# Routing's small operations shared out over a whole step of the groups, and the rows' last turns put earlier

## The chip, the cores and the metric

The kernel runs on one core of a Trainium2 chip. The metric is the device time of one execution in microseconds (us); three executions of the kernel before gave 1698.09, 1701.14 and 1708.59 us, median 1701.14 us. Engine names are those of the profile: PE (TensorE), DVE (VectorE), ACT (ScalarE), POOL (GpSimd) and SP (SyncE).

## The reference

Eight sequences of 5056 positions by 128 channels are convolved along the sequence with one filter `h`, by real FFTs of twice the length. The result, 40,448 tokens of 128, then goes through a mixture of experts with two-level routing:

```python
y = irfft(rfft(x, n=2*S, axis=1) * rfft(h, n=2*S, axis=0)[None], n=2*S, axis=1)[:, :S]
t = y.reshape(B*S, D)
g_logits = t @ w_group                       # 4 groups: take the largest, softmax weight g_w
e_logits = t @ w_expert[g]                   # 4 experts of that group: largest, softmax weight e_w
out[tok] = g_w * e_w * (relu(t[tok] @ w1[g, e]) @ w2[g, e])    # hidden size 1024, one expert per token
```

All inputs and results are float32.

## The kernel before

The convolution is a two-step Fourier transform (158 by 64 points) written as matmuls, in three rounds (`ROUNDS`): the filter and sequences 0 and 1, then sequences 2 to 4, then 5 to 7. A round has a first stage (`stage1`, 96 pieces: matmuls L419 and L426, copies and adds L437 to L443 into the resident tile `st`) and a stage of groups (`groups`). The groups come in pairs of frequencies, 40 pairs in 20 steps of two pairs. In a step PE transforms both pairs (`forward`, L520), DVE multiplies each by the filter's spectrum in two operations (`multiply`, L538: `y`, then `m`) and adds the two (`add`, L572; on POOL in the first round), and PE transforms back the two pairs of the step before (`inverse`, L588), which ACT copies into `zs` (L598) and SP stores to `zd`. Forward and inverse results share three double banks of PSUM (`pp`), which turn in order: an inverse whose bank held a forward result waits until DVE's `m` has read it.

Beside rounds 1 and 2 runs the last transform and the routing of the round before (`side`), and beside the expert blocks that follow the three rounds that of round 2. Its unit is a batch of 8 of the 64 positions. For each: two lumps (`lump`: matmuls L722 and L736 into the banks `py0` and `py1`, copied by ACT into `yT`, L743); the logits' matmuls (`lm`, L789, copied into `lT`, L794); their transposes (`lt`, L799, copied into `lg`, L803); three or four turns of rows (`rows`: transposes of `yT`, L779, copied by ACT into the rows `rw`, L780); and 41 steps of the routing's small operations, eight of them empty (`gate_math`, L895 to L986, nearly all on DVE, with four small matmuls L972 and L973). `lm`, `lt` and `rows` take `py0` and `py1` in turn, the same two banks as the lumps. The finished rows are sent to their expert's place in `srt` by single indirect transfers on POOL (`scatter`, L855), each after a tiny cast of its positions on DVE or ACT (L854).

The order of all instructions on each engine is written by hand. `run` makes one list, `main`, of (weight, function). In the groups a step is 11 entries with the weights `GW = [0, 0, 0, 0, 0, 0, 2.0, 0, 0, 0, 2.0]`; in the first stage each piece weighs 0.45, with entries of weight 0 between some. `weave` goes through `main` and, at entries that weigh something, puts in as much of the side's work as is due by its own times `t` (in slots; a batch in rounds 1 and 2 lasts 8 slots, so a slot is about half a step of the groups). Steps marked small are not put in at once but held in a list, `light`, and at each entry of weight 0 a part of them is issued:

```python
room[i] = room[i + 1] + 1 if main[i][0] == 0 else 0
...
    if w == 0:
        flush(-(-len(light) // room[i]))
```

So before the change `room[i]` is the number of weight-0 entries left in the present run of such entries, and the held steps are all out before the next weighted entry: what came due at the entry with index 6 goes out over the three entries 7 to 9, what came due at index 10 over the next six. The forwards and multiplies stand at indexes 1 to 5, the adds at 5, the inverses at 7 and 8, lumps and rows behind 6 and 10.

Of the kernel before, what the change touches and what calls it, by code (L numbers as in the profile page):

```python
# [45 lines left out]
GW = [0, 0, 0, 0, 0, 0, 2.0, 0, 0, 0, 2.0]  # L46
# [124 lines left out]
    }  # L171


def weave(main, sides):


    light = []

    def flush(n):
        for f in light[:n]:  # L180
            f()
        del light[:n]

    room = [0] * (len(main) + 1)
    for i in reversed(range(len(main))):
        room[i] = room[i + 1] + 1 if main[i][0] == 0 else 0
    for i, (w, f) in enumerate(main):
        f()
        if w == 0:
            flush(-(-len(light) // room[i]))  # L190
        for s in sides:
            if s["start"] <= i < s["end"]:
                if i == s["start"]:
                    s["done"] = 0
                    s["acc"] = s["sacc"] = 0.0
                    s["len"] = sum(w for w, _ in main[s["start"]:s["end"]])
                    s["total"] = sum(x[0] for x in s["steps"])
                s["acc"] += w / s["len"]
                while s["done"] < len(s["steps"]) and (s["sacc"] < s["acc"] * s["total"] - 1e-6 or i == s["end"] - 1):
                    sw, sf, small = s["steps"][s["done"]]  # L200
                    if small and room[i + 1] > 0 and i < s["end"] - 1:
                        light.append(sf)
                    else:
                        if small:
                            flush(len(light))
                        sf()
                    s["sacc"] += sw
                    s["done"] += 1
                if i == s["end"] - 1:
                    flush(len(light))  # L210
# [18 lines left out]
class Kernel:  # L229
# [455 lines left out]
    def side(self, r):  # L685
# [80 lines left out]
        def rows(i):  # L766

            if i == 0:
                od["rw"] = []
                od["o"] = od.get("o", -1) + 1  # L770
                while self.sends and self.sends[0][0] < 8 * r + od["o"] - 1:
                    self.send()
            if i % 2 == 0:
                od["rw"].append(cx.tile([128, RH, ROW], F32, name="rw", bufs=4))
            n = min(4, T - 4 * i)
            pt = bank()
            for j in range(n):
                k = (4 * i + j) * GP
                nc.tensor.transpose(out=pt[:, j * D:(j + 1) * D], in_=self.yT[:, k:k + GP], identity=self.ident)  # L779
            nc.scalar.copy(  # L780
                out=od["rw"][i // 2][:, 4 * i % RH:4 * i % RH + n, 0:D], in_=pt[:, 0:n * D].rearrange("p (j d) -> p j d", d=D)
            )
# [26 lines left out]
        def advance(g):  # L809
            return lambda: next(g, None)  # L810

        def both(*fs):
            return lambda: [f() for f in fs]
# [3 lines left out]
        for o in range(N2 // 8):  # L817
            math = {}
            ops = self.gate_math(od, math, b0 * S + o * 8, T, nu, REST if r < 2 else REST2)
            sends = [self.scatter(math, k, GP if k < T - 1 else last, r, T) for k in range(T)]  # L820
            if r < 2:
                t = 8 * o
                at.append((t, lump(2 * o), False))
                at.append((t + 3, lump(2 * o + 1), False))
                at.append((t + 4.7, both(lm, lambda: rows(0)), False))
                at.append((t + 6.4, both(lt, lambda: rows(1)), False))
                at.append((t + 9.5, both(*more), False))
                at += [(t + 6.5 + 5.6 * k / (NMATH + REST), advance(ops), True) for k in range(NMATH + REST)]
                at.append((t + 12.15, lambda o=o, s=sends: self.sends.extend((8 * r + o, f) for f in s), True))
            else:  # L830

                t = 6 * o
                at.append((t, lump(2 * o), False))
                at.append((t + 2, lump(2 * o + 1), False))
                at.append((t + 3, both(lm, lambda: rows(0)), False))
                at.append((t + 4, both(lt, lambda: rows(1)), False))
                at.append((t + 5, both(*more), False))
                at += [(t + 4.02 + 3.3 * k / (NMATH + REST2), advance(ops), True) for k in range(NMATH + REST2)]
                at.append((t + 7.4, lambda o=o, s=sends: self.sends.extend((8 * r + o, f) for f in s), True))
# [758 lines left out]
    def run(self):  # L1598
        tc = self.tc
        with ExitStack() as ctx:  # L1600
            self.pools(ctx)
            with ExitStack() as c2:
# [10 lines left out]
                def add(f, w=0.0):  # L1613
                    main.append((w, f))
# [17 lines left out]
                for r in range(3):  # L1632
                    if r == 1:
                        add(self.share)
                    pre, steps = gr[r]
                    rest = late(r - 1) if r > 0 else []
                    n = len(s1[r][1])
                    t0 = self.table_0()
                    for k, f in enumerate(s1[r][1]):
                        add(f, W_S1)  # L1640
                        if r > 0 and k % 2 == 1:
                            add(self.send)
                        if r == 0:
                            add(advance(more))
                        if r == 2 and ("end", 0) in mark:
                            add(advance(t0))
                        if k >= 1:
                            for g in rest[RP * k - RP:RP * k]:
                                add(g)
                        if k == SIDE0 and r > 0:  # L1650
                            add(side[r - 1][0])
                        if k == max(SIDE0 + SIDEG, END0 if r == 2 else 0) and r > 0:
                            mark["start", r - 1] = len(main)
                            if r == 2:
                                mark["end", 0] = len(main)
                        if k >= n - PRE and (k - n) % 5 == 0:
                            add(advance(pre))
                    if r > 0:
                        add(lambda: None, W_END)
                    for p in range(0, NQ, 2):  # L1660
                        for w, f in steps[p // 2]:
                            add(f, w)
                        if p >= NQ - LOAD1:
                            add(advance(s1[r + 1][0] if r < 2 else early))
                add(turn)
                add(lambda: self.ffn_first(0))
                rest = late(2)
# [3 lines left out]
                for k, f in enumerate(steps):  # L1671
# [35 lines left out]
                        add(lambda i=m * n // TAKE: self.take(i))  # L1707
                weave(main, [
                    dict(start=mark["start", r], end=mark["end", r], steps=side[r][1]) for r in range(3)
                ])  # L1710
                self.ffn_tail()


# [25 lines left out]
```

## Time and profile before

| | before |
|---|---|
| timed runs, median (lowest, highest) | 1701.14 us (1698.09, 1708.59) |
| profiled execution, own time / span | 1700.13 us / 1698.3 us |
| PE busy | 1630.5 us, 96% of the span |
| DVE busy | 1302.5 us, 77% |
| ACT busy | 1046.8 us, 62% |
| POOL busy | 773.3 us, 46% |
| mean granted clock of PE | 0.991 |

By the lines at work the profile falls into these stretches: the first round to about 137 us; then round 1's first stage to 200 us and its groups to 357 us; round 2's first stage to 445 us and its groups, with the turn to the experts, to 625 us; then expert blocks to the end. A wait row names engine, tile and line, what was waited for, the total in us, how many times, and the longest. A timeline row has the start in us, the duration in us, the instruction, and in brackets the idle time before it and what ended that.

### The profile page before, as it was taken

The page shows a single profiled execution, that of the slowest core. Times are in us where ns is not written, and L with a number is a line of the kernel's source. Part 1 is how long each engine was busy: PE and PEld are TensorE (multiplying, and loading weights), DVE is VectorE, ACT ScalarE, POOL GpSimd, SP SyncE. Part 2 cuts the span into 40 slices and gives each one's busy share as a digit, 9 for nine tenths or more (in the row PEclk, how much of TensorE's full clock was granted, in tenths as well). Part 3 has the DMA queues.
Part 4 walks back from the last instruction along what each step waited for, and adds up shares of the span by engine and source line. Part 5 has one row for each costly group of instructions (what it writes and reads, how often), then busy time and mean ns, then how long its engine had stood idle before and what let it go on. Part 6 is the DMA issues. An engine that isn't in the chain of part 4 may idle for free. (4 is left out here: it accounts for less than half of the span.)

```text
span 1698.3 us, 50924 instructions
## 1 busy us (share of the span) xinstructions
PE 1630.5 (96%) x18317; PEld 1275.8 (75%) x18317; DVE 1302.5 (77%) x3092; ACT 1046.8 (62%) x2461; POOL 773.3 (46%) x742
## 2 busy tenths in 40 slices
PE   8998999989899989999999999999999999999996
PEld 7676755557665557888778887888888888879986
DVE  6554698975788886777777788888887787878875
ACT  5564544544545456666666676777777776657764
POOL 1452233442555553254554454446565663334443
PEclk9999999999999999999999999999999999999998
DMA  7797678888798976566655544567555774444554
GB/s 210 224 295 223 191 243 263 274 245 217 200 289 280 287 227 172 165 177 179 177 164 173 158 139 129 153 197 219 161 161 152 213 220 139 126 132 145 164 160 139
DMA packets 278001, 330.36 MB, mean 195 GB/s; under 512 B 31863, under 2 KB 210304, under 8 KB 277720
## 3 DMA queue, kind: packets, MB, share of 16 engines
q1 hardware_dynamic: 248856, 270.93, 54.6%
q0 software_dynamic: 20608, 41.79, 7.2%
q10 hardware_dynamic: 8256, 14.10, 3.0%
q8 instruction: 152, 2.49, 0.7%
q14 instruction: 129, 1.06, 0.2%
HBM read 230.35 MB, written 96.86 MB: 193 GB/s over the span
## 5 line engine op out<-in xcount | busy, mean ns | idle before, releaser
L855 POOL DMA_INDIRECT srt<-rw,pos x320 | 345.3, 1079 | 391.4 <-DVE pos L854 116.2
L1422 POOL DMA_INDIRECT out<-orow,at x176 | 187.8, 1067 | 254.1 <-ACT at L1420 226.8
L1422 POOL DMA_INDIRECT out<-orow,sids x92 | 94.1, 1022 | 126.1 <-DVE orow L1389 89.4
L538 DVE TENSOR_TENSOR y<-pp,hg 128x768 f32<-128x768 f32 (+1 forms) x120 | 103.6, 864 | 54.3 <-ACT hg L528 32.3
L598 ACT COPY zs<-pp 128x768 f32<-128x768 f32 (+1 forms) x118 | 85.3, 723 | 81.0 <-PE pp L588 40.5
L588 PE MATMUL pp<-y,cg 64*64 64x384 f32 (+1 forms) x1472 | 116.4, 444 | 12.1 <-DVE m L538 8.0
L1357 DVE SCALAR_TENSOR_TENSOR h0l<-px,h0h 128x512 fp32r<-128x512 f32 (+1 forms) x109 | 73.7, 676 | 59.3 <-ACT h0h L1356 58.4
L520 PE MATMUL pp<-st,cg 64*64 64x192 f32 (+1 forms) x1556 | 114.4, 404 | 1.2 <-PE pp L520 0.6
L1356 ACT ACTIVATE h0h<-px 128x512 fp32r<-128x512 f32 (+1 forms) x109 | 63.9, 587 | 80.6 <-PE px L1353 72.5
L438 DVE TENSOR_TENSOR st<-pp,odd 128x320 f32<-128x320 f32 x96 | 46.9, 489 | 77.2 <-ACT odd L437 76.9
L538 DVE TENSOR_TENSOR m<-pp,hg 128x768 f32<-128x768 f32 (+1 forms) x120 | 102.9, 857 | 2.1 <-ACT hg L530 2.1
L1357 DVE SCALAR_TENSOR_TENSOR h2l<-px,h2h 128x512 fp32r<-128x512 f32 (+1 forms) x112 | 75.5, 674 | 31.0 <-ACT h2h L1356 29.9
L588 PEld LDWEIGHTS pp<-y,cg 64*64 64x64 f32 x1472 | 55.4, 133 | 52.4 <-issue 27.6
L722 PEld LDWEIGHTS py<-ig,zm 126*64 126x64 f32 x2048 | 75.0, 139 | 24.6 <-issue 8.2
L743 ACT COPY yT<-py 128x474 f32<-128x474 f32 (+1 forms) x96 | 44.3, 514 | 77.3 <-PE py L736 70.9
L1357 DVE SCALAR_TENSOR_TENSOR h3l<-px,h3h 128x512 fp32r<-128x512 f32 (+1 forms) x111 | 74.6, 672 | 22.5 <-ACT h3h L1356 21.0
L722 PE MATMUL py<-ig,zm 126*64 126x79 f32 x2048 | 83.2, 237 | 8.0 <-DMA zm<-zd 4.7
L520 PEld LDWEIGHTS pp<-st,cg 64*64 64x64 f32 x1556 | 59.0, 133 | 41.1 <-issue 32.5
L572 POOL TENSOR_TENSOR y<-y,m 128x512 f32<-128x512 f32 x40 | 50.8, 1274 | 76.8 <-DVE m L560 43.3
L1356 ACT ACTIVATE h3h<-px 128x512 fp32r<-128x512 f32 (+1 forms) x111 | 65.3, 588 | 29.1 <-PE px L1353 24.4
L1357 DVE SCALAR_TENSOR_TENSOR h1l<-px,h1h 128x512 fp32r<-128x512 f32 (+1 forms) x111 | 74.7, 673 | 4.2 <-ACT h1h L1356 0.3
L1356 ACT ACTIVATE h1h<-px 128x512 fp32r<-128x512 f32 (+1 forms) x111 | 65.2, 587 | 17.0 <-PE px L1353 14.6
(476 smaller groups left out, 5151.7 us busy)
## 6 DMA issues: line engine op xcount, KB each, us to landing
wr<-in_moe_w SPq DMA_DIRECT2D x373, 256.0 KB
zd<-zs SPq DMA_DIRECT2D x78, 384.0 KB
zm<-zd SPq DMA_DIRECT2D x64, 378.0 KB
cg<-in_c_g SPq DMA_DIRECT2D x102, 224.0 KB
xr<-srt SPq DMA_DIRECT2D x71, 260.0 KB
hg<-hd SPq DMA_DIRECT2D x80, 128.0 KB
zd<-zs SPq DMA_DIRECT2D x39, 256.0 KB
xt<-in_x ACTq DMA_DIRECT2D x54, 160.0 KB
```

The costliest lines, as they stand in the source:

```text
L438: nc.vector.tensor_tensor(out=all_st[:, 0:2 * HALF, d], in0=even, in1=odd, op=ALU.add)
L520: nc.tensor.matmul(px[c * 64:c * 64 + 64, b, to], lhsT=k, rhs=data[:, of], start=begin, stop=i == len(steps) - 1 or p == 0 and i == 1, til ...
L538: nc.vector.tensor_tensor(out=t[:, :, 0:w].rearrange("p t (r u d) -> p t r u d", r=2, u=nu), in0=taken(px, part).unsqueeze(1).broadcast_to ...
L572: (nc.gpsimd if r == 0 else nc.vector).tensor_tensor(out=y[:, :, 0:w], in0=y[:, :, 0:w], in1=m[:, :, 0:w], op=ALU.add)
L588: nc.tensor.matmul(pz[c][h:h + 64, 0:w], lhsT=wt[c * 64:c * 64 + 64, k + h:k + h + 64], rhs=y[c * 64:c * 64 + 64, part, 0:w], start=part = ...
L598: nc.scalar.copy(out=z[:, 0:n, 0:w], in_=pp[:, 0:n, 0:w])
L722: nc.tensor.matmul(pys[q][c:c + 64, col(n, u)], lhsT=zms[q][:, n % QB, k:k + 64], rhs=self.ig[:, 0:NH], start=n % QB == 0 and u == 0, stop ...
L743: nc.scalar.copy(out=self.yT[:, k:k + QB * c1], in_=pys.pop(q)[:, 0:QB * c1])
L855: ins = self.nc.gpsimd.indirect_dma_start(out=self.srt, out_offset=bass.IndirectOffsetOnAxis(ap=k["pos"][0:p, j:j + 1], axis=0), in_=k["rw ...
L1356: nc.scalar.activation(out=hh, in_=p, func=AF.Relu)
L1357: nc.vector.scalar_tensor_tensor(out=hl, in0=p, scalar=0.0, in1=hh.bitcast(F32), op0=ALU.max, op1=ALU.subtract)
L1422: ins = self.nc.gpsimd.indirect_dma_start(out=self.a["out"], out_offset=bass.IndirectOffsetOnAxis(ap=ids, axis=0), in_=o, in_offset=None, ...
```

## The change

Two edits. In `weave`, for entries ahead of the expert blocks (`turn` is the list's index there), `room[i]` becomes the number of weight-0 entries among the next 11 (one step of the groups), wherever these are more than 5. There, held small steps are no longer all issued before the next weighted entry; each weight-0 entry issues a ninth or so of what is held, and some carry over. In `side`, for rounds 0 and 1 of the side's work, `lt` with the second turn of rows moves from 6.4 to 5.8 slots after the batch's start, the remaining turns of rows from 9.5 to 7.4 (ahead of the next batch's first lump at 8, where they stood between its first lump at 8 and its second at 11), and the small steps begin at 5.9 in place of 6.5.

```diff
-def weave(main, sides):
+def weave(main, sides, turn):
...
     for i in reversed(range(len(main))):
         room[i] = room[i + 1] + 1 if main[i][0] == 0 else 0
+    for i in range(turn):
+        near = sum(w == 0 for w, _ in main[i:min(i + len(GW), turn)])
+        room[i] = near if near > len(GW) // 2 else room[i]
...
                 at.append((t + 4.7, both(lm, lambda: rows(0)), False))
-                at.append((t + 6.4, both(lt, lambda: rows(1)), False))
-                at.append((t + 9.5, both(*more), False))
-                at += [(t + 6.5 + 5.6 * k / (NMATH + REST), advance(ops), True) for k in range(NMATH + REST)]
+                at.append((t + 5.8, both(lt, lambda: rows(1)), False))
+                at.append((t + 7.4, both(*more), False))
+                at += [(t + 5.9 + 5.6 * k / (NMATH + REST), advance(ops), True) for k in range(NMATH + REST)]
...
+                mark["turn"] = len(main)
                 add(turn)
...
                 weave(main, [
                     dict(start=mark["start", r], end=mark["end", r], steps=side[r][1]) for r in range(3)
-                ])
+                ], mark["turn"])
```

Line numbers in the changed kernel are 3 higher from `weave` on (L722 becomes L725), 4 higher at the end.

The first place is PE's order in round 2's groups, one and the same batch: L588 is an inverse, L779 the third and fourth turn of rows, L520 the next two forwards, L722 the next lump. Before:

```order
L588 MATMUL pp<-y,xt_83 64x384 x8
L588 MATMUL pp<-y,xt_84 64x384 x8
L779 MATMUL py_9680<-ident,yT 128x128 x4
L779 MATMUL py_9686<-ident,yT 128x128 x3
L520 MATMUL pp<-st,cg 64x384 x4
L520 MATMUL pp<-st,cg 64x192 x4
L520 MATMUL pp<-st,ns 64x192 x4
L520 MATMUL pp<-st,cg 64x384 x4
L520 MATMUL pp<-st,cg 64x192 x4
L520 MATMUL pp<-st,ns 64x192 x4
L722 MATMUL py_9753<-ig,zm 64x79 x12
L722 MATMUL py_9771<-ig,zm 64x79 x12
```

With the change the same two turns (now L782) stand a lump earlier:

```order
L591 MATMUL pp<-y,cg 64x384 x16
L782 MATMUL py_9480<-ident,yT 128x128 x4
L782 MATMUL py_9486<-ident,yT 128x128 x3
L725 MATMUL py_9491<-ig,zm 64x79 x12
L725 MATMUL py_9509<-ig,zm 64x79 x12
```

The two turns were followed by two forwards and then the batch's second lump; now the first lump stands right behind them, with no matmul of the groups between. Over the two rounds' groups the last rows stand right ahead of a lump five times (three in round 1, two in round 2; never before), and at two places `lm`, `lt` and rows, or `lt` and both rows, follow each other with no forward or inverse between.

The second place is ACT's order around the copies of those same two turns (L780): L598 copies an inverse's result, L903 is the exponential that the routing takes of `td`, which DVE computes (L897), L743 copies a lump's result. Before:

```order
L598 COPY zs<-pp 128x768
L854 CAST pos<-posf 128x1
L956 CAST tot<-cs 128x16
L780 COPY rw<-py_9680 128x4x128
L780 COPY rw<-py_9686 128x3x128
L530 ACTIVATE hg<-hg 128x128 x2
```

With the change:

```order
L601 COPY zs<-pp 128x768
L857 CAST pos<-posf 128x1
L906 ACTIVATE te<-td 128x60
L783 COPY rw<-py_9480 128x4x128
L783 COPY rw<-py_9486 128x3x128
L746 COPY yT<-py_9491 128x474
```

The copies stood behind a cast of the batch's totals and stand now right behind that exponential, so ACT comes to them once DVE has done `td`.

The third place is DVE's order at the end of round 2's groups: L572 is an add, L538 the multiplies of the last step (`y`, then `m`), everything else a small step of the last batch. Before, from the second add on:

```order
L572 TENSOR_TENSOR y<-y,m 128x768
L897 TENSOR_TENSOR td<-el,tmx 128x60
L899 SCALAR_TENSOR_TENSOR tm<-td,wt_150 128x60
...
L958 SCALAR_TENSOR_TENSOR wp<-gs,es 128x15
L964 TENSOR_SCALAR rw<-ids_118 128x8
L966 RECIPROCAL rw<-wp 128x8
L964 TENSOR_SCALAR rw<-ids_118 128x7
L538 TENSOR_TENSOR y<-pp,hg 128x768
L854 CAST pos<-posf 128x1
L966 RECIPROCAL rw<-wp 128x7
L538 TENSOR_TENSOR m<-pp,hg 128x768
```

With the change:

```order
L575 TENSOR_TENSOR y<-y,m 128x768
L908 TENSOR_REDUCE tq<-tm 128x15
L910 TENSOR_TENSOR eo<-tm,tq 128x60
...
L961 SCALAR_TENSOR_TENSOR wp<-gs,es 128x15
L541 TENSOR_TENSOR y<-pp,hg 128x768
L857 CAST pos<-posf 128x1
L967 TENSOR_SCALAR rw<-ids_118 128x8
L969 RECIPROCAL rw<-wp 128x8
L541 TENSOR_TENSOR m<-pp,hg 128x768
L967 TENSOR_SCALAR rw<-ids_118 128x7
L969 RECIPROCAL rw<-wp 128x7
```

Between the add and the next `y` stood 14 small steps and stand 9 now. Of the five others two went ahead of the add, two behind `y` and one behind `m`; the second reciprocal (L966, now L969) went from ahead of `m` to behind it. The order on SP doesn't change at all, that on POOL by where a few memsets stand among the scatters. The multiplies, matmuls and transfers are the same in number and size.

## The prediction

> **What bounds the kernel now.** I read the page's busy shares, then the table by stretch, then PE's waits in the two stretches of groups that the change reorders, then the timelines around the longest waits.
>
> ```profile
> PE 1630.5 (96%) x18317; PEld 1275.8 (75%) x18317; DVE 1302.5 (77%) x3092; ACT 1046.8 (62%) x2461; POOL 773.3 (46%) x742
> ```
>
> By stretch (length, then busy us of PE, PEld, DVE, ACT and POOL with counts, granted clock, DMA share, GB/s):
>
> ```profile
> 137.00:200.00 63.00, 56.63 (x1496) 45.83 (x1490) 32.01 (x101) 30.44 (x69) 12.27 (x16) 0.97 0.77 214
> 200.00:357.00 157.00, 149.25 (x2581) 90.81 (x2581) 139.13 (x344) 74.14 (x203) 59.68 (x55) 1.00 0.81 251
> 357.00:445.00 88.00, 79.00 (x2002) 63.64 (x1996) 54.64 (x218) 40.18 (x88) 36.94 (x41) 0.96 0.78 214
> 445.00:625.00 180.00, 169.10 (x2778) 103.51 (x2775) 155.97 (x377) 88.80 (x241) 103.16 (x95) 0.98 0.86 265
> 625.00:1698.00 1073.00, 1048.70 (x6651) 875.56 (x6650) 838.04 (x1881) 736.57 (x1660) 506.44 (x476) 0.99 0.56 165
> ```
>
> PE is the bound everywhere. The change reorders only the first four rows; there PE idles 6.4 + 7.8 + 9.0 + 10.9 = 34 us, 2% of the span. That caps any gain, and most of it is not the routing's: the first stages' idle time (rows 1 and 3) is largely waits for loads. In the groups DVE is close behind PE, 139 of 157 us and 156 of 180. What PE waits for there, first 200 to 357 us:
>
> ```profile
> PE pp L588 <- DVE m L538: 4.5, 7, 1.2
> PE py L722 <- ACT rw L780: 1.3, 1, 1.3
> PE pp L588 <- DVE off L976: 0.2, 1, 0.2
> ```
>
> and 445 to 625 us:
>
> ```profile
> PE pp L588 <- DVE m L538: 3.4, 3, 2.6
> PE py L722 <- ACT rw L780: 1.9, 2, 1.0
> PE ptr L1306 <- DVE base L977: 1.3, 1, 1.3
> PE pp L588 <- DVE wp L958: 1.0, 1, 1.0
> PE pp L588 <- DVE td L897: 0.3, 1, 0.3
> PE pp L520 <- DVE m L538: 0.2, 1, 0.2
> ```
>
> So waits on DVE, which the sharing out is about, come to 4.5 + 0.2 + 3.4 + 1.3 + 1.0 + 0.3 + 0.2 = 10.9 us, and waits of a lump for the copy of rows, which the earlier rows are about, to 3.2 us in three cases. The longest is at the end of round 2's groups. DVE:
>
> ```profile
> 606.26 0.95 DVE L572 TENSOR_TENSOR y<-y,m 128x768 f32<-128x768 f32 x1
> 607.13 0.22 DVE L897 TENSOR_TENSOR td<-el,tmx 128x60 f32<-128x60 f32 x1
> ...
> 610.33 0.43 DVE L964 TENSOR_SCALAR rw<-ids 128x7 f32<-128x7 f32 x1
> 610.43 0.96 DVE L538 TENSOR_TENSOR y<-pp,hg 128x768 f32<-128x768 f32 x1
> 611.31 0.14 DVE L854 CAST pos<-posf 128x1 int32<-128x1 f32 x1
> 611.37 0.19 DVE L966 RECIPROCAL rw<-wp 128x7 f32<-128x7 f32 x1
> 611.48 0.91 DVE L538 TENSOR_TENSOR m<-pp,hg 128x768 f32<-128x768 f32 x1
> ```
>
> and PE:
>
> ```profile
> 605.40 1.20 PE L520 MATMUL pp<-st,cg 64*64 64x384 f32 x16
> ...
> 608.43 1.52 PE L588 MATMUL pp<-y,cg 64*64 64x384 f32 x16 [0.21 <-ACT zs L598]
> 612.53 2.34 PE L588 MATMUL pp<-y,cg 64*64 64x384 f32 x16 [2.58 <-DVE m L538]
> ```
>
> Between add and `y` stand 14 small steps, 607.13 to 610.43: 3.3 us in which DVE does nothing for PE, and the second inverse, whose bank `m` must free, stands 2.58 us.
>
> **Part by part.** *Sharing out.* It removes no work; it moves small steps behind multiplies. Only what moves from ahead of the awaited `m` to behind it shortens a wait. At this place that is two steps (third place of the order): 0.43 and 0.19 us by their rows, so 2.58 becomes 2.0 at best; the 14 were due within that step anyway. At a mid-stretch wait, 238.31 us, more moves. PE and the ten small steps ahead of its multiplies, with their first and last row:
>
> ```profile
> 232.63 0.43 DVE L930 TENSOR_TENSOR oh<-go,eo 128x160 f32<-128x160 f32 x1
> ...
> 234.43 0.16 DVE L966 RECIPROCAL rw<-wp 128x2 f32<-128x2 f32 x1
> ```
> ```profile
> 237.16 0.17 PE L973 MATMUL pp<-spare,ones 128*128 128x16 bf16 x1
> 238.31 1.52 PE L588 MATMUL pp<-y,cg 64*64 64x384 f32 x16 [0.98 <-DVE m L538]
> ```
>
> Those ten took 1.9 us; the changed order has eight there, but two more behind `y`, and carries some to later steps: I take 0.4 to 0.8 us off such a wait. Over the 15 waits, ten of them large enough to give 0.4, that is -4 us. The bounds: -10.9 if all go; +2 if the steps newly put between `y` and `m` (about one more at ten places, 0.2 us each) delay more than the shorter runs save.
>
> *Rows ahead of the lump.* The copies' price shows where it stalled before:
>
> ```profile
> 459.87 0.98 PE L779 MATMUL py<-ident,yT 128*128 128x128 f32 x7
> 464.71 1.04 PE L722 MATMUL py<-ig,zm 126*64 126x79 f32 x24 [0.84 <-ACT rw L780]
> ```
> ```profile
> 463.14 0.25 ACT L903 ACTIVATE te<-td 128x60 f32<-128x60 f32 x1 [3.43 <-DVE td L897]
> 464.07 0.97 ACT L780 COPY rw<-py 128x512 f32<-128x512 f32 x2
> ```
>
> The rows were transposed by 460.85, but their copies began at 464.07, because ACT stood 3.43 us at the exponential, in front of them in its queue, waiting for DVE's `td`. Two forwards lay between rows and lump and hid all but 0.84. With the change nothing lies between them at five turns. Behind an ACT that is free the lump waits for the first copy, about 0.5 (half of 0.97 for two); behind one held as above it would wait 464.07 - 460.85 + 0.5 = 3.7. At two of the five (the batch of the first two places of the order, and one in round 1) the exponential stands right ahead of the copies. There `td` follows a step's adds, as at 607.13 us above, and so comes late. I take 1.6 us each there, an estimate from the lower half of 0.5 to 3.7, since at both an inverse pair runs on PE between the step's forwards and the rows and gives DVE that time; 0.5 at two; and nothing at the fifth, where the rows' only bank is the one the lump takes second. That is 4.2. The other five turns keep a pair of forwards or inverses ahead of the lump; three of ten such cost 3.2 before, so five cost 1.6. Together 5.8 against 3.2 before: +2.6. Bounds: -3.2, if the copies are always in time, and 5 x 3.7 + 1.6 - 3.2 = +17.
>
> Where `lm`, `lt` and rows, or `lt` and both rows, now follow each other, each transpose waits for the copy ahead of it: half of 0.97 at two places, +1 (0 to 2). In the first stages the rows have half as many matmuls as before between them and the lump: +0.5 (0 to 2) for four batches.
>
> *The filler moves.* The 0.98 us of the two turns leaves the stretch between a batch's two lumps, where PE waits for DVE, and goes where PE is ahead anyway. In the step above PE has forwards of 2.8 us (605.40 to 608.22) and two inverses of 1.5, with the rows 6.8; DVE has six large operations at 0.87 (606.26 to 607.13) and the run of 3.3, 8.5 at least. Without the rows PE has 5.8, and waits that much sooner. Each round's groups have a step of this kind in the middle, with no lump, and the banks in hand take up part of it: +0.7 in all. Bounds: 0, and 0.98 for each of round 2's five batches and half of it for round 1's six, +8.
>
> *What is queued behind.* Nothing on SP moves; POOL's scatters keep their order. The DVE casts that feed them (0.14 us) move with the rest.
>
> The sum: -4 + 2.6 + 1 + 0.5 + 0.7 = +0.8 us, on the execution of 1700.13 gives 1701; the median of the runs, 1701.14, is 1.0 above that execution, so 1702.
>
> *The clock.* After some waits PE ran at half its clock:
>
> ```profile
> 366.60:370.00 3.40, 3.40 (x62) 0.61 0.83 261
> 612.50:619.30 6.80, 5.44 (x36) 0.54 0.70 224
> ```
> ```profile
> 365.24 1.18 PE L588 MATMUL pp<-y,cg 64*64 64x384 f32 x6 [1.44 <-issue]
> 345.15 1.31 PE L722 MATMUL py<-ig,zm 126*64 126x79 f32 x32 [1.28 <-ACT rw L780]
> ```
>
> The last figure but two is the clock: 0.61 for 3.4 us behind the wait of 1.44, worth 3.4 x 0.39 = 1.3 us, and 0.54 for 6.8 us behind that of 2.58, worth 3.1. Behind the wait of 1.28 there is none (200 to 357 us is at 1.00). So a wait beyond about 1.4 us costs 1.3 to 3.1 more; in the sum I count none gained or lost, since 2.58 only falls to 2.0 and the new ones stand at 1.6 and below. [...] The trace shows half clock behind 1.44 and 2.58 us, so I go by the rows.
>
> **The rivals.** *Sharing out works in full.* If the waits come from the order within a step rather than DVE's load, all 10.9 go, and with the 2.58 the 3.1 of clock: 1701.1 - 10.9 - 3.1 + (2.6 + 1 + 0.5 + 0.7) = 1692. For it: DVE idles in these stretches (18 and 24 us), so there is room. Against: from 606 to 612 us, in the rows above, it has no gap.
>
> *Slower: the lump stands behind ACT's queue.* At each of the five turns the copies are held as at 463 us: 3.7 each and 1.3 of clock, 25 us, with 1.6 for the other five, less the 3.2 of before, less the 4 of the sharing, plus 2.2 of the rest: +21.6, 1723. With two held, which is likelier, it is 2 x 5.0 + 1.0 + 1.6 - 3.2 - 4 + 2.2 = +7.6, 1709. It decides from the point where DVE does `td` later than the transposes end by more than 1.4 us. For it: three of ten turns were held so before. Against: at two of the five the exponential is not ahead of the copies.
>
> *The move does nothing.* DVE's load per batch sets the pace between lumps, and the same steps wait elsewhere: 1701 to 1702, inside the forecast.
>
> **How the numbers follow.** Forecast, 1697 to 1706 with 1702 the likeliest: 0.64 (the third rival in it). Full sharing, about 1692: 0.16. Held rows, about 1709: 0.17, and all five, 1723: 0.03. A measurement of this kernel tells about 1% (17 us) from no change. Full sharing with all rows in time besides reaches 1701.1 - 10.9 - 3.1 - 3.2 + 2.2 = 1686, short of the 1684 that is faster by 1%: 0.02 for what I don't see. Slower by over 1% needs the 1723: 0.03. The rest, 0.95, is within 1%. The range takes in the faster case and the two held turns: 1691 to 1711.
>
> **What would show it.** Right: PE's waits `pp L588 <- DVE m` in the two groups fall from 7.9 us to about 4, `py L722 <- ACT rw` (now L725, L783) grow from 3.2 to about 6, PE's idle time in the four stretches stays near 34, and the stretch from 625 us on keeps its 1073. Wrong on the sharing: the `m` waits keep their sum or vanish. Wrong on the rows: the waits for `rw` stay under 3, or pass 10 with half clock behind them. The forecast as a whole would be wrong if the expert blocks, whose order the change leaves alone, took another time.

## The result and the profile after

The changed kernel takes 1713.08 us (median of 22 runs, 1703.51 to 1718.35), the kernel before 1702.06 us in the runs beside it (median of 22, 1696.25 to 1711.47): ratio 1.0055, 95% interval 1.0042 to 1.0067. So it is slower by 0.55%, 9 us by the ratio and 11 between the medians, where 1702 was forecast with a range to 1711. The profiled execution of the changed kernel took 1714.82 us, its span is 1712.8 us.

The busy line of the changed kernel's page: the engines did what they did before, in a longer span.

```profile
PE 1635.0 (95%) x18317; PEld 1278.1 (75%) x18317; DVE 1299.4 (76%) x3092; ACT 1046.1 (61%) x2461; POOL 772.7 (45%) x742
```

The table by stretch, cut where each kernel's own stages begin: round 1's first stage, its groups, round 2's first stage, its groups, the experts (length, busy us of PE, PEld, DVE, ACT, POOL, granted clock, DMA share, GB/s). Before:

```profile
139.16:210.18 71.02, 64.40 (x1738) 52.97 (x1738) 38.22 (x130) 33.50 (x77) 15.10 (x19) 0.98 0.72 200
210.18:361.45 151.27, 144.52 (x2363) 85.32 (x2361) 136.04 (x319) 71.10 (x194) 57.17 (x52) 1.00 0.82 258
361.45:447.43 85.98, 76.98 (x1963) 62.38 (x1962) 52.05 (x216) 40.26 (x90) 35.69 (x40) 0.96 0.81 219
447.43:617.42 169.99, 159.09 (x2715) 98.38 (x2714) 149.30 (x362) 81.37 (x223) 98.78 (x92) 0.99 0.86 267
617.42:1698.30 1080.88, 1056.29 (x6689) 879.49 (x6688) 842.85 (x1891) 742.40 (x1674) 510.10 (x479) 0.99 0.57 166
```

After:

```profile
140.52:217.43 76.91, 64.53 (x1739) 52.83 (x1739) 38.24 (x130) 33.29 (x77) 14.96 (x19) 0.98 0.64 185
217.43:368.92 151.49, 144.85 (x2365) 85.84 (x2362) 134.74 (x316) 71.85 (x196) 54.92 (x51) 1.00 0.81 256
368.92:455.17 86.25, 77.25 (x1961) 63.23 (x1960) 50.70 (x216) 39.42 (x88) 35.48 (x40) 0.94 0.80 219
455.17:635.04 179.87, 163.65 (x2716) 100.50 (x2715) 149.23 (x366) 80.45 (x222) 99.10 (x91) 0.97 0.82 251
635.04:1712.80 1077.76, 1056.16 (x6689) 878.82 (x6688) 842.42 (x1889) 742.81 (x1674) 511.88 (x481) 0.99 0.57 166
```

Two stretches grew: round 1's first stage by 5.9 us, round 2's groups by 9.9. Round 1's groups and round 2's first stage are where they were within 0.3 us, and the experts are 3 us shorter. The four stretches together are 16.3 us longer, the whole span 14.5: this execution is 1.7 us above its kernel's median, that of before 1.9 below its own. PE's idle time in the first four went from 6.6 + 6.8 + 9.0 + 10.9 = 33 to 12.4 + 6.6 + 9.0 + 16.2 = 44 us. In round 2's groups PE's busy time grew as well, 159.09 to 163.65 for the same matmuls, at a clock of 0.97 for 0.99.

PE's waits of the changed kernel from 140 to 640 us, those for copies of rows and for DVE's `m`:

```profile
PE py L725 <- ACT rw L783: 9.2, 8, 2.3
PE pp L591 <- DVE m L541: 7.3, 9, 1.8
PE py L725 <- DMA zm<-zd: 4.9, 2, 3.3
PE pp L975 <- DVE m L541: 1.8, 1, 1.8
PE pp L591 <- DVE td L900: 1.2, 1, 1.2
```

The waits for rows went from 3.2 us in three to 9.2 in eight. Those for `m`, 8.0 over the whole run before, are 7.3 + 1.8. The prediction's place, PE first, then ACT:

```profile
521.19 0.98 PE L782 MATMUL py<-ident,yT 128*128 128x128 f32 x7
524.46 2.21 PE L725 MATMUL py<-ig,zm 126*64 126x79 f32 x48 [2.29 <-ACT rw L783]
```
```profile
523.53 0.25 ACT L906 ACTIVATE te<-td 128x60 f32<-128x60 f32 x1 [1.32 <-DVE td L900]
523.82 0.97 ACT L783 COPY rw<-py 128x512 f32<-128x512 f32 x2
```

The rows were transposed by 522.17; ACT stood at the exponential until 523.5, copied the rows behind it, and the lump began 2.29 us late. Behind it the clock halved. Of the stretches at half clock ahead of the experts these are the last two of the changed kernel's six; the other four are 3.4 us each. Before had three of 3.4 and one of 6.8, the one that the prediction shows at the end of round 2's groups:

```profile
526.00:532.80 6.80, 6.80 (x102) 4.51 (x103) 1.51 (x5) 1.42 (x4) 0.77 (x2) 0.51 0.89 215
631.80:638.60 6.80, 5.85 (x30) 2.21 (x23) 4.63 (x12) 3.19 (x7) 3.40 (x3) 0.51 0.53 164
```

That is 4 x 3.4 + 2 x 6.8 = 27.2 us after, 3 x 3.4 + 6.8 = 17.0 before, each worth half: 5.1 us more in this execution. The 6.8 us from 526.00 are new and stand behind the new wait of 2.29. Over the 22 runs of the changed kernel the mean granted clock is 0.9895; in the runs of the kernel before beside the experiments it is 0.991. That makes the clock's part 0.0015 x 1713, some 2.6 us, in the mean, an estimate that takes in the experts too.

In the first stage of round 1 the same thing happens on a smaller scale (PE, then ACT):

```profile
179.66 0.44 PE L782 MATMUL py<-ident,yT 128*128 128x128 f32 x2
...
182.90 1.31 PE L725 MATMUL py<-ig,zm 126*64 126x79 f32 x32 [1.49 <-ACT rw L783]
```
```profile
182.02 0.24 ACT L906 ACTIVATE te<-td 128x40 f32<-128x40 f32 x1 [1.82 <-DMA xt<-in_x]
182.47 0.38 ACT L783 COPY rw<-py 128x256 f32<-128x256 f32 x1
```
```profile
181.72 0.20 DVE L900 TENSOR_TENSOR td<-el,tmx 128x40 f32<-128x40 f32 x1
```

The rows end at 180.1 and are copied at 182.47, behind an exponential that comes at 182.02. (The row names a load as its releaser, but the `td` that it reads was computed by DVE only at 181.72, the third fence.) One piece of the first stage (L422, 0.78 us) stands between rows and lump, and it is too short to hide this. The waits for rows are 2.4 us of the 5.8 us by which PE's idle time grew in this stage.

### The profile page after: what moved, and what is told of

It reads as the page before. It is cut to its first block, busy times and chain, and to the rows that moved or that the text cites. A ratio compares the mean times of both kernels' runs of the same rounds, so it can differ in the third digit from the quotient of the medians.

```text
span 1712.8 us, 50911 instructions
## 1 busy us (share of the span) xinstructions
PE 1635.0 (95%) x18317; PEld 1278.1 (75%) x18317; DVE 1299.4 (76%) x3092; ACT 1046.1 (61%) x2461; POOL 772.7 (45%) x742
## 5 line engine op out<-in xcount | busy, mean ns | idle before, releaser
L725 PE MATMUL py<-ig,zm 126*64 126x79 f32 x2048 | 85.3, 240 | 17.2 <-ACT rw L783 9.2
L725 PEld LDWEIGHTS py<-ig,zm 126*64 126x64 f32 x2048 | 76.8, 141 | 32.8 <-ACT rw L783 12.1
```

The source lines that it names most:

```text
L725: nc.tensor.matmul(pys[q][c:c + 64, col(n, u)], lhsT=zms[q][:, n % QB, k:k + 64], rhs=self.ig[:, 0:NH], start=n % QB == 0 and u == 0, stop ...
```

## The experiments

The expectations use letters: A, the lumps stand behind ACT's copies of rows (A1: because the exponential ahead of them in ACT's queue waits for DVE); B, sharing out is itself what costs; C, the stretch between two lumps lost its filler, or the earlier small steps cost; D, waits only move. All runs are full kernels with the reference's computation, timed in five rounds against the kernel before on the same chip.

### One part alone

**share_only**, the sharing with the times of before:

```diff
-                at.append((t + 5.8, both(lt, lambda: rows(1)), False))
-                at.append((t + 7.4, both(*more), False))
-                at += [(t + 5.9 + 5.6 * k / (NMATH + REST), advance(ops), True) for k in range(NMATH + REST)]
+                at.append((t + 6.4, both(lt, lambda: rows(1)), False))
+                at.append((t + 9.5, both(*more), False))
+                at += [(t + 6.5 + 5.6 * k / (NMATH + REST), advance(ops), True) for k in range(NMATH + REST)]
```

> The sharing out alone; rows and small steps begin at their old times (6.4, 9.5, 6.5). Theory A, lumps stand behind ACT's copies of the rows: no row is moved, so the loss is gone and the sharing's own effect shows, ratio 0.995 to 1.001 to the kernel before (-8 to +2 us), py waits for rw near the 3.2 us of before. Theory B, the sharing itself costs, because small steps now stand between the multiplies: ratio 1.004 or more (+7 us and up). Theory C, the stretch between a batch's lumps has lost its filler: like A, ratio at most 1.001, since the rows still lie in that stretch.

Measured: 1692.92 us, ratio 0.9955 (0.9935 to 0.9976). **rows_only**, the new times with the old sharing (the three lines on `room` that the change adds to `weave` are taken out):

> The rows and the small steps' begin at the new times (5.8, 7.4, 5.9), the old sharing. The last rows stand right ahead of a lump five times in the two groups, as in the changed kernel. Theory A: ratio 1.005 to 1.010, py waits for rw 7 us or more. Theory B: 0.999 to 1.002. Theory C: 1.005 to 1.010 too, but with the gain in waits of pp for DVE's m, and py waits for rw under 5 us.

Measured: 1724.43 us, 1.0150 (1.0124 to 1.0176), more than any of the theories had expected, with 15.6 us of waits for rows. So B falls: the sharing gains, and what loses is in the times. The two parts are not independent. The new times cost 1.5% with the old sharing and 1.0% with the new (0.9955 to 1.0055, some 17 us), and the sharing gains 0.45% at the old times and 0.95% at the new.

### How far ahead the rows stand

**share_apart** is the change with the last rows at 6.9 in place of 7.4 slots, where they are never right ahead of a lump in the groups; **touching** has them at 7.95. There its trace shows them right ahead of a lump nine times in the groups (its expectation says ten) and three times in the first stages; in the change it is five times, all in the groups:

```diff
-                at.append((t + 7.4, both(*more), False))
+                at.append((t + 6.9, both(*more), False))    # share_apart; touching: 7.95
```

> The changed kernel, with the last turns of rows at 6.9 slots in place of 7.4: in no batch of the groups do they stand right ahead of a lump, and they still lie outside the stretch between a batch's lumps. Theory A: most of the loss goes, ratio at most 1.002 to the kernel before, py waits for rw under 4 us. Theory B: 1.004 to 1.007, as the changed kernel. Theory C: 1.004 to 1.007, with py waits for rw under 4 us.

> The changed kernel, with the last turns of rows at 7.95 slots: they stand right ahead of a lump ten times in the two groups, in place of five. Theory A: the loss grows by half to twice, ratio 1.008 to 1.013, py waits for rw 12 us or more. Theories B and C: 1.004 to 1.007, as the changed kernel.

Measured: 1703.52 us, 1.0024 (1.0007 to 1.0041) with 2.5 us of waits for rows, and 1717.67 us, 1.0112 (1.0085 to 1.0140) with 15.9. The waits go with the number of lumps that follow the rows at once, and so does the time. But share_apart has no more of these waits than before and is still 0.6 to 0.7% behind the sharing alone, over the 1.002 that A allowed; its `m` waits are 8.2 + 2.0 us, those of share_only 3.8 + 0.7. So there is a second loss, from what else was put earlier.

### The exponential out of the copies' way

**exp_later** is the change with the exponential issued two small steps later, when DVE has `td`:

```diff
-            nc.scalar.activation(out=e, in_=d, func=AF.Exp)
             yield
             nc.vector.tensor_reduce(out=q, in_=m, axis=AX.X, op=ALU.max)
             yield
+            nc.scalar.activation(out=e, in_=d, func=AF.Exp)
             nc.vector.tensor_tensor(out=o, in0=m, in1=b4(q), op=ALU.is_equal)
```

> The changed kernel with the routing's exponential issued on ACT two small steps later, so that it no longer stands right ahead of the last rows' copies at the batches where a lump follows them directly; rows and lumps stay where the change puts them. Theory A1, the copies are late because ACT stands at the exponential waiting for DVE: a third to a half of the loss goes, ratio to the kernel before 1.001 to 1.004, py waits for rw 4 to 6 us. Theory A2, the copy's own time behind the transposes is the wait, whatever stands ahead: 1.005 to 1.006, waits for rw 8 us or more.

Measured: 1705.23 us, 1.0043 (1.0017 to 1.0068). The waits for rows fell from 9.2 to 2.7 us as A1 has it, and further; the ratio's interval overlaps the change's, so the time alone settles nothing here. The same edit on the sharing alone, **share_exp**:

> The sharing alone (rows and small steps at their old times) with the exponential two small steps later. A1: the three waits for rw that the kernel before has too go as well, ratio 0.992 to 0.995, under the 0.9955 of the sharing alone. A2: 0.9955 within 0.002.

Measured: 1691.08 us, 0.9964 (0.9943 to 0.9984), waits for rows 1.8 us. The time is the one that A2 expected, not A1: nothing is seen to be gained where the copies are held for a short time only.

To see the price of the held copies in time, the edit was made where they are held longest: **rows_only_2** is rows_only again, **rows_exp** the same with the exponential later.

> The new times of rows, logits' transposes and small steps with the old sharing, again, as the yardstick of rows_exp. Both theories: 1.013 to 1.018 of before, waits of a lump for rw 14 to 17 us over the run, about 40 us of half clock ahead of the expert blocks (the run before had 1.0150, 15.6 us and 44 us).

> rows_only_2 with the exponential issued two small steps later, so that it comes to ACT's queue when DVE has td; all matmuls, copies and times are the same. Theory A (the lump stands behind ACT's held copies, and this is lost time): the waits for rw fall from 15.6 us to under 6, half clock from 44 us to under 30, and the time falls by 10 us of waits and 7 us of clock, to 1.003 to 1.008. Rival D (the waits move: a lump that doesn't wait for rw waits for the next thing, since DVE's load per batch or the small steps' early start set the pace): the rw waits fall as much, but others grow in their place, and the time stays at 1.011 to 1.017.

Measured on one chip: 1725.28 us, 1.0169 (1.0139 to 1.0199), and 1708.15 us, 1.0056 (1.0037 to 1.0075). Between the two, from their runs' means, 0.9886 (0.985 to 0.992): 17 us between the medians from moving one kind of small instruction, twice in a batch, in ACT's queue. One batch in both; rows_only_2, PE and ACT:

```profile
563.47 0.98 PE L779 MATMUL py<-ident,yT 128*128 128x128 f32 x7
568.54 1.72 PE L722 MATMUL py<-ig,zm 126*64 126x79 f32 x22 [4.09 <-ACT rw L780]
```
```profile
567.50 0.25 ACT L903 ACTIVATE te<-td 128x60 f32<-128x60 f32 x1 [4.96 <-DVE td L897]
567.90 0.97 ACT L780 COPY rw<-py 128x512 f32<-128x512 f32 x2
```

and rows_exp (where some matmul records of the rows are missing):

```profile
549.78 0.60 PE L779 MATMUL py<-ident,yT 128*128 128x128 f32 x4
550.73 1.86 PE L722 MATMUL py<-ig,zm 126*64 126x79 f32 x48 [0.35 <-ACT rw L780]
```
```profile
550.09 0.97 ACT L780 COPY rw<-py 128x512 f32<-128x512 f32 x2 [1.49 <-PE py L779]
556.09 0.24 ACT L906 ACTIVATE te<-td 128x60 f32<-128x60 f32 x1
```

ACT now waits for PE's rows in place of PE for ACT's copies. PE's waits for rows over the stages, of rows_only_2 and then of rows_exp:

```profile
PE py L722 <- ACT rw L780: 16.7, 8, 4.1
```
```profile
PE py L722 <- ACT rw L780: 5.1, 5, 2.4
```

11.6 us of waits went, and of 47.8 us at half clock ahead of the experts 23.9 were left, worth 12.0 us (the clock of the four stretches was 0.96, 0.99, 0.94 and 0.93 in rows_only_2, 0.98, 1.00, 0.94 and 0.97 in rows_exp); the two spans differ by 21.5. Little took their place: all the waits in the full lists of the two kernels come to 52.2 and 42.3 us, so D falls for these waits. One of the two longest stretches at half clock in rows_only_2 begins at the end of the wait of 4.09 above:

```profile
567.70:578.00 10.30, 9.46 (x124) 6.59 (x128) 4.01 (x15) 3.28 (x9) 1.97 (x3) 0.51 0.46 116
```

In the changed kernel itself, **change_3** and **exp_later_3**:

> The changed kernel again, as the yardstick of the next: 1.004 to 1.007 of before, waits of a lump for rw 6 to 10 us.

> The change with the exponential two small steps later. If the held copies carry the loss in the changed kernel, it is 0.4 to 0.8% faster than change_3 (6.5 us of waits and about as much of clock). If they carry little there because the lump would wait for the next thing anyway, it is within 0.2% of change_3.

Measured on one chip: 1707.13 us, 1.0059 (1.0037 to 1.0082), and 1703.02 us, 1.0035 (1.0012 to 1.0058); between the two 0.9975 (0.995 to 1.000). So in the changed kernel the held copies carry about a quarter of a per cent, at the edge of what this measures. PE's waits from 140 us to the experts, change_3 and then exp_later_3:

```profile
PE py L725 <- ACT rw L783: 8.2, 8, 2.3
PE pp L591 <- DVE m L541: 7.7, 9, 1.8
```
```profile
PE pp L591 <- DVE m L541: 7.7, 9, 1.8
PE py L725 <- ACT rw L783: 3.2, 5, 1.0
```

The waits for `m` stay. Round 1's first stage is 77.1 us in change_3 (76.9 in the changed kernel's first profile) and 69.3 in exp_later_3 (71.7 in exp_later): moving the exponential takes its loss away, more than the 2.1 to 2.4 us of waits for rows that went with it. In change_3 the clock is part of it (0.93 in this stage, 1.00 in exp_later_3); in the first profile of the change it is not (0.98, as before). Round 2's groups are 176.6 and 176.2 us here (179.9 and 172.1 in the first two profiles of these kernels), against 166.4 in share_only_2 (below): of their loss the later exponential gives back a part at most.

Both were also run on a chip where every kernel, the one before included, took about 5% longer (before 1786.83 us; **change_again**, **exp_later_again**):

> The changed kernel once more, to stand beside the later exponential on the same chip. Both theories: ratio to the kernel before 1.0055 within its interval, py waits for rw 7 us or more, and near 27 us of half clock ahead of the expert blocks if the first profile was typical.

> The changed kernel with the exponential two small steps later, once more. A1 (copies late because ACT stands at the exponential): ratio under that of the changed kernel beside it by 0.002 or more, py waits for rw at most 4 us. A2 (the wait is the copy's own time): the same within 0.001.

Measured: 1805.10 us, 1.0107 (1.0068 to 1.0146), and 1804.18 us, 1.0081 (1.0043 to 1.0118). The change loses about twice as much on that chip, which its expectation did not have. The two ratios are as far apart as on the other chip, but here their intervals overlap widely, so nothing is shown by it.

### The steps put earlier

Three kernels start from share_only and move one thing more. **share_lt_early** moves the logits' transposes with the second turn of rows; **share_math_early** moves these and the small steps (with both row tiles taken at the batch's first turn); **share_more_early** moves the last rows alone:

```diff
-                at.append((t + 6.4, both(lt, lambda: rows(1)), False))
+                at.append((t + 5.8, both(lt, lambda: rows(1)), False))   # share_lt_early, share_math_early
-                at.append((t + 9.5, both(*more), False))
+                at.append((t + 7.4, both(*more), False))                 # share_more_early
-                at += [(t + 6.5 + 5.6 * k / (NMATH + REST), ...
+                at += [(t + 5.9 + 5.6 * k / (NMATH + REST), ...          # share_math_early
```

> The sharing with the logits' transposes and the second turn of rows at 5.8 slots and nothing else moved (rows 9.5, small steps from 6.5). If the transposes' place is what loses in share_math_early, 0.999 to 1.002 of before. If it is the earlier small steps, 0.993 to 0.998, as the sharing alone.

> The sharing, with the logits' transposes at 5.8 and the small steps from 5.9 slots, but the last turns of rows left at 9.5 (both row tiles are taken at the first turn, so that the small steps find them). It tells what the rest of the loss is, that the rows at 6.9, ahead of no lump, still had (1.0024 against 0.9955 of the sharing alone). If the earlier small steps cost it: ratio 1.000 to 1.003. If the rows' matmuls are missed between a batch's lumps: 0.995 to 0.997.

> The sharing, with the last turns of rows alone at 7.4 slots, the logits' transposes and the small steps at their old times; the rows stand right ahead of a lump twice in round 2's groups. If the earlier small steps cost the rest: ratio 0.996 to 0.999. If the missing filler does: 1.001 to 1.005.

Measured: 1694.80 us, 0.9978 (0.9964 to 0.9993); 1697.13 us, 1.0004 (0.9987 to 1.0020); 1709.51 us, 1.0073 (1.0048 to 1.0099). The first two make a ladder with the others, each against its own runs of before: sharing 0.9955, transposes earlier 0.9978, small steps earlier too 1.0004, the last rows at 6.9 besides 1.0024, at 7.4 (the change) 1.0055, at 7.95 1.0112. Up to 1.0024 the intervals of neighbours overlap, so only two rungs together are told apart; from there each lies clear of the next, the change of share_apart only just. PE's waits on DVE in the two rounds' groups climb with it: 6.4 us with the sharing alone (share_only_2, below), 7.1 with the transposes earlier, 9.6 with the small steps too, 10.7 in the change. share_math_early and share_apart differ by the place of the last rows alone (and by when the rows' buffers are taken). There the `m` waits go from 6.9 to 10.2 us, with no more rows right ahead of a lump: one sign that the rows' matmuls were missed between a batch's two lumps. By these two ratios it is some 0.2%, which their intervals don't tell from nothing.

share_more_early missed its expectation. Its last rows stand right ahead of a lump five times in the groups, as in the change, and right behind `lt` and the second turn at two more places, with no forward or inverse between. Its waits for rows are 8.3 us in six, almost those of the change.

Was earlier the fault, or any other place? **share_math_late** (on the slower chip) and **share_math_late_2** have the small steps from 7.1 to 12.1 slots, beside **share_only_2**:

```diff
-                at += [(t + 6.5 + 5.6 * k / (NMATH + REST), advance(ops), True) for k in range(NMATH + REST)]
+                at += [(t + 7.1 + 5.0 * k / (NMATH + REST), advance(ops), True) for k in range(NMATH + REST)]
```

> The sharing alone, with the small steps from 7.1 to 12.1 slots in place of 6.5 to 12.1; rows and transposes at their old times. If the earlier small steps (5.9) cost because they press on DVE where PE waits for it, later ones gain: ratio 0.991 to 0.995. If the place of the small steps matters little: 0.9955 within 0.0015. If denser small steps cost more than their later begin saves: 0.997 or more.

> The sharing alone, rows and small steps at the old times, again. If the gain of 0.45% was real it comes out at 0.993 to 0.998 here too; if it was that chip's, at 0.998 to 1.004.

> The sharing, rows at the old times, the small steps of the routing due from 7.1 to 12.1 slots (6.5 to 12.1 in share_only). If the small steps lose by standing close behind the logits' transposes, so that a step comes to DVE before what it needs is there, this is as fast as share_only_2 or faster by up to 0.3%. If what costs is any crowding of them (the same number in 5.0 slots where 5.6 were), it is slower than share_only_2 by 0.3 to 1%, as share_math_early was by 0.5%.

Measured: share_math_late 1803.77 us, 1.0094 (1.0064 to 1.0124), with no sharing alone beside it on that chip; share_only_2 1691.31 us, 0.9955 (0.9939 to 0.9970); share_math_late_2 1704.14 us, 1.0024 (1.0004 to 1.0044). So a later and narrower spread loses too, 0.7% against share_only_2 (1.0074, 1.0055 to 1.0093), and the nearness to the transposes can't be its reason. The expectation put this down to crowding, 5.0 slots for 5.6. That isn't shown: the start moved with the width, and the waits of its round 2 groups are spread over many kinds, the largest 2.8 us for `m` and 2.7 for rows.

Sharing alone, at the times of before, has the lowest ratio of the study, the same on two chips (with the later exponential, share_exp, it is not told apart from it). Its groups in share_only_2, against 151.27 and 169.99 us before, and PE's longest waits for DVE in them, of the first groups and then of the second:

```profile
210.76:358.34 147.58, 143.97 (x2369) 85.61 (x2365) 134.18 (x315) 70.79 (x194) 55.22 (x50) 1.00 0.82 264
447.71:614.09 166.38, 158.66 (x2715) 97.49 (x2714) 147.98 (x360) 80.56 (x220) 95.78 (x89) 0.99 0.87 270
```
```profile
PE pp L591 <- DVE m L541: 1.3, 1, 1.3
...
PE pp L591 <- DVE m L541: 3.1, 2, 2.5
PE ptr L1309 <- DVE base L980: 1.4, 1, 1.4
```

## Why the prediction was wrong

**The step that failed: what the new times cost.** The prediction's sum gives them +2.6 + 1 + 0.5 + 0.7 = +4.8 us. The runs show 1.0%, some 17 us, with the new sharing in place (0.9955 to 1.0055). About half of it is from `lt` at 5.8 and the small steps from 5.9 slots, whose move had no term beyond the packed places and was taken to be neutral: these two alone go from 0.9955 to 1.0004, 8 us, while PE's waits on DVE in the groups rise from 6.4 to 9.6 us. The other half, 1.0004 to 1.0055, comes with the last rows at 7.4, where the terms for rows, filler and clock were too small.

**Sharing out, -4 us.** For the sharing alone the direction and the mechanism were right, and the size too small in time. In the groups the waits on DVE were 10.9 us; in share_only_2 they are 1.3 + 3.1 + 1.4 and three of 0.2, 6.4: a fall of 4.5, and in time 7 us. In the changed kernel they are 7.3 + 1.8 + 1.2 and one of 0.4, 10.7, so the fall is gone. Yet the sharing gains in the changed kernel too, 0.95% against rows_only, and by another way: the waits for rows are 9.2 us there for the 15.6 of rows_only, while those on DVE in the groups, 7.6 in rows_only, are longer. Why they grow where both parts meet isn't traced.

**Rows ahead of the lump, +2.6 us.** The place and the cause were right and the size somewhat too small: in the groups 1.1 + 5.7 = 6.8 us for 3.2, +3.6. The lump behind the exponential in round 2 waited 2.29 us where 1.6 was taken. The argument that an inverse pair on PE gives DVE the time didn't hold: DVE came to `td` after an add:

```profile
522.16 0.95 DVE L575 TENSOR_TENSOR y<-y,m 128x768 f32<-128x768 f32 x1
...
523.27 0.22 DVE L900 TENSOR_TENSOR td<-lg,tmx 128x60 f32<-128x60 f32 x1
```

Another lump waited 1.69 us, at 558.19, with no late `td`. ACT:

```profile
555.44 0.80 ACT L601 COPY zs<-pp 128x768 f32<-128x768 f32 x1 [2.67 <-DMA zd<-zs]
...
557.13 0.31 ACT L533 ACTIVATE hg<-hg 128x128 f32<-128x128 f32 x1 [0.54 <-DMA hg<-hd]
...
557.55 0.97 ACT L783 COPY rw<-py 128x512 f32<-128x512 f32 x2
```

It had stood for a store of `zs` to drain, and then for a load of the filter, both ahead of the copies. So an ACT that isn't held by the exponential isn't free, and the 0.5 for such turns was too low at this place.

**First stages, +0.5 us.** Round 1's waited 1.49 and 0.95 for rows, +2.4, the same mechanism, outside the prediction's count of five. With the exponential later these waits go and the first stage of round 1 is 69.3 to 71.7 us, in place of 76.9 and 77.1; what else went with them is not traced.

**Clock, 0.** The text said that the new waits would stand at 1.6 and below and that none would count, though its own bound was about 1.4. With 2.29 it was 5.1 us more in the profiled execution, of which 3.4 stand behind that wait (0.51 for the 6.8 us from 526.00) and the rest is not traced to a wait of the change; in the mean of the runs it is some 2.6, the estimate above. A bound on the length of a wait was the wrong measure besides: one of 1.49 us has no half clock behind it and one of 1.48 has 6.8 us, as the last section shows.

**Filler moved, +0.7, and packed places, +1.** Neither has a wait of its own in the trace. The nearest that the runs come is share_apart against share_math_early: 3.3 us more of `m` waits and some 0.2%, within the intervals.

In sum, for the profiled execution: waits on DVE -0.2, waits for rows 3.6 + 2.4 = 6.0, clock 5.1, together 10.9 us, for the +0.8 of the prediction. A wait for `zm` grew by 1.9 (3.0 to 4.9) but stands at 3.3 in share_only_2's first stage as well, so isn't shown to be the rows'. The four stretches grew by 16.3 us, so some 3 us are in none of these; that 10.9 is near the 11.0 between the medians is luck.

**The rivals.** "The lump stands behind ACT's queue" with two held, at 1709, was the nearest: the queue was what it said, with one long wait and seven short ones rather than two long ones. It had 0.17. What it left out as well is the cost of the earlier `lt` and small steps. "Sharing works in full", 1692, is what share_only measured, for a change that moves no rows. Of what was to show it, the expert blocks kept their length to within 3 us, the rows' waits did grow, to 9.2 rather than 6, while `m` kept its sum and the idle time went to 44 us. The prediction took a kept sum of `m` for a sign against the sharing; the experiments show that the sharing gained all the same, and that the times lost more.

**What stays open.** Why 6.5 slots is a good start for the small steps and 5.9, or 7.1 with less room, are not; and why round 2's groups stay 6 to 10 us above the sharing alone with the later exponential. One thing that differs there is DVE's wait for what ACT does to the filter (L533, L530 before), of the changed kernel and of before:

```profile
DVE m L541 <- ACT hg L533: 5.5, 5, 1.8
```
```profile
DVE m L538 <- ACT hg L530: 2.1, 2, 1.7
```

The filter stands in the same queue as the copies, and `m` behind it. No run took that away by itself.

## What to carry to other kernels

A copy that frees a bank for the next matmul stood here behind what ACT had been given first (3.4 us in rows_only_2), so before moving one look at what stands ahead of it on its engine, not only at what the matmul engine has in hand: exponentials of 0.25 us that wait for another engine cost 17 us in rows_only_2, where they stood ahead of the copies, and a quarter of a per cent in the changed kernel. Test such a change part by part, since here a gain of 0.45% and two losses of about 0.5% came in one edit. Sharing small work evenly between the awaited operations paid; starting it earlier, or later in less room, did not. And give every part that an edit moves a term in the sum, also one that seems neutral: here some half a slot without a price was half of what the new times cost.

## What the runs showed of the hardware

Ahead of the experts the granted clock was 0.50 in four stretches of 3.41 us and two of 6.83 in the trace of the changed kernel, and in three of 3.41 and one of 6.82 in that of before; the stretch of rows_only_2 above is 10.30 us at 0.51. What stood behind a wait differed: 6.8 us at half clock behind the 2.29, those 10.3 behind the 4.09 of rows_only_2, and none behind the 1.49 up to 182.90 (1.00 from 181.60 to 188.40), where the same wait in change_3, 1.48 us up to 181.35, has this behind it:

```profile
181.60:188.40 6.80, 6.80 (x136) 5.86 (x136) 2.99 (x14) 1.98 (x6) 0.00 (x0) 0.54 0.81 224
```

Half clock doesn't begin at a fixed time behind a wait: at 525.82 it is 1.36 us behind the end of the 2.29 (524.46), in change_3 at 182.14 0.79 behind that of the 1.48. What differed is how long PE was busy in the 3.4 us around the wait. The two equal waits above, in the changed kernel and in change_3, and then the one of 2.29, the last two up to where half clock begins:

```profile
181.07:184.49 3.42, 1.93 (x72) 1.68 (x67) 2.84 (x11) 1.15 (x4) 0.00 (x0) 1.00 0.37 120
178.73:182.14 3.41, 1.57 (x54) 1.44 (x56) 2.79 (x12) 1.15 (x4) 0.00 (x0) 1.00 0.44 138
522.41:525.82 3.41, 1.36 (x40) 1.36 (x42) 1.71 (x6) 1.22 (x3) 2.68 (x3) 1.00 0.06 20
```

PE was busy 56% of the first, with no half clock behind it, and 46 and 40% of the other two; its idle time together is 1.49 us in the first and 1.84 and 2.05 in the others. So in these three cases half clock goes with the idle time of the whole stretch, and the length of the single wait, 1.49 and 1.48 us, doesn't tell the first two apart. Three cases give no bound, and why it is so is not shown.

In the rows shown ACT keeps its order: copies whose input had been ready for 3.4 us (564.45 to 567.90) stayed behind an exponential that had waited 4.96 us for `td`.

On one chip the four kernels timed there took 5 to 6% longer (before 1786.83 us for 1702.06, the change 1805.10 for 1713.08), with many short waits of PE that the profile puts down to nothing, here the longest such line of change_again:

```profile
PE pp L422 <- issue: 13.4, 27, 1.5
```

What they are wasn't tried.
